# No weight remainders on GpSimd, ranks and weight addresses ahead of the row numbers, an own tile for the first two gathers

## The chip, the cores and the metric

The kernel runs on one core of one Trainium2 chip. The metric is device time in microseconds (us) of one execution. A profile gives the span of an execution too, which is a little shorter than its time. TensorE is called PE below, VectorE DVE, ScalarE ACT and GpSimd POOL, as in the profile; SP is the engine that issues most DMAs.

## The reference

Three stages follow each other: attention, a mixture of experts that sends every token to one expert, and a gated feed-forward block.

```python
# 1 attention: q, k, v are [2, 8, 576, 64]
scores = q @ k.T / 8
scores = where(scores >= max(scores) - tau, scores, -1e9)
x = (softmax(scores) @ v)              # heads joined: 1152 tokens x 512

# 2 mixture of experts: 8 experts, w1 [8, 512, 1024], w2 [8, 1024, 512]
logits = x @ w_gate                    # 1152 x 8
e = argmax(logits); gate = softmax(logits)[e]
# each expert takes its tokens in order, up to `capacity` (288)
y = relu(x_e @ w1[e]) @ w2[e]
x = gate * y[back at the token's place]     # dropped tokens are 0

# 3 feed-forward
out = (silu(x @ w_gate2) * (x @ w_val)) @ w_out
```

## The kernel before

**Stages.** Attention ends near 165 us of the span, routing takes until about 175.8 us, the experts run until about 322 us and the feed-forward block takes the rest. Inside routing and the experts the order of instructions on PE, ACT, DVE and POOL is the order in which the code is written; only SP is left to a scheduler.

**Weights.** Every expert has four loads of 1 MB (`w1` group 0 and 1, `w2` group 0 and 1), issued by SP (`next_raw`) into a raw buffer. There are three buffers `raw` and, once the experts begin, two more `rawx`. Each load gives two pieces. `next_piece` takes a piece from the raw buffer into one of six slots `ring`, as two float32r halves: the high part is a rounded copy (`split_hi`, line 220 on ACT or 218 on POOL), the low part is what the rounding left (`finish`, line 312, source minus high part, on DVE or POOL). A low part on DVE is put off until the next call; after the second piece of a load its buffer is free and SP may fill it again. The table `POOLED` names pieces whose two halves POOL makes: `w2` pieces 1 and 3 of experts 1 and 2, four pieces.

**Experts 0, 1 and 2.** Experts are taken in order of their token counts, the smallest first: expert 0 with 64 rows, 1 and 2 with 128, the others with more. For 1 and 2 (`expert_rows`, line 1443) PE does eight products of six matmuls of 512 columns each, one per piece: four with `w1`, then four with `w2`. Between them it turns the hidden rows (`turn`: ACT copies `hb` out of PSUM, PE transposes, ACT and DVE write the two parts of `ht`), turns the result of the expert before (`yb`, `yT`), and transposes one tile of gathered tokens at a time (`sort_tile`, line 1333, into `xsT`). After each product `next_piece` is called.

**Routing.** From the expert chosen for each of 1152 tokens (nine tiles of 128) the kernel needs four things.

- The place of each token in sorted order: `pos`, `dst`, `ndlo`, from prefix counts that PE adds up in `pt_`. The last matmul into `pt_` adds `gc`, the number of tokens of smaller experts.
- The tokens' row numbers `ids`: nine one-hot tables `olo` and nine matmuls into `ps_i`. Two gathers (indirect DMAs on POOL, line 1213) then fetch the first two tiles of sorted rows, into a raw buffer called `gbuf`, which goes back to the weights once both tiles are used; seven more gathers follow after the branch.
- Expert 0's 64 rows, without a gather: nine one-hot tables `hot` (lines 1159 to 1167, one on DVE, four on POOL, four on ACT) pick them by matmul into `ps_x0` (`pick_rows`, line 1178), eight matmuls in two groups per half of a tile.
- The rank of each expert (`rank`, `rm`, `vals`), which a matmul turns into `info`: which expert is the r-th and where its rows begin. SP reads `info` to address the weights of expert 1. From `info` also comes `slack`, on whose value all engines branch to one of several table widths (line 1773); and from `grhs` and a matmul into `ps_gt` comes `gat`, the gates in sorted order.

Of the kernel before, what the change touches and what calls it, by code (L numbers as in the profile page):

```python
# [10 lines left out]
F32 = mybir.dt.float32  # L11
# [12 lines left out]
def attention_moe_swiglu_kernel(  # L24
# [15 lines left out]
    nc = tc.nc  # L40
# [45 lines left out]
    XE = ()  # L86
    POOLED = tuple((e, "w2", g) for e in (1, 2) for g in (1, 3))
    MORE = ((1, 3), (2, 3))
# [22 lines left out]
    POLO = (8,)  # L111
    VH, PH, AH = (8,), (0,1,2,3), (4,5,6,7)
    SNAP = 1.5 * 2.0 ** 30
# [168 lines left out]

    slots, pooled = {}, set()

    def next_piece(lo_eng=None, hi_eng=None):
# [10 lines left out]
        if nm in ("w1", "w2"):  # L296
# [4 lines left out]
            if e in halves:  # L301
                src = t[:, (g % 2) * NPC:(g % 2 + 1) * NPC].rearrange("p (k f) -> p k f", k=kk)
            if (e, nm, g) in POOLED and pooled:
                lo_eng = hi_eng = nc.gpsimd
            lo_eng = lo_eng or nc.vector
# [831 lines left out]
    for a, (l, r_) in enumerate(rows_):  # L1137
# [5 lines left out]
                           op1=ALU.add)  # L1143
    V.scalar_tensor_tensor(out=gc, in0=krow, scalar=key[:, 0:1], in1=cntc.to_broadcast(T8),
                           op0=ALU.is_gt, op1=ALU.mult)
    pt_ = ps_r[:, 0:NTL * NE].rearrange("p (t e) -> p t e", t=NTL)
# [8 lines left out]
    mm(pt_[:, 0:M4], same, pre3, start=False, stop=False)  # L1155
    mm(pt_, onef, gc.unsqueeze(1).to_broadcast([NE, NTL, NE]), start=False, stop=True)
    V.tensor_scalar(out=npos, in0=p0_, scalar1=-1.0, scalar2=None, op0=ALU.mult)
    for t in VH:
        V.tensor_scalar(out=hot[:, t], in0=iot[:, 0:PK], scalar1=npos[:, t:t + 1],
                        scalar2=gm[:, t:t + 1], op0=ALU.is_equal, op1=ALU.mult)  # L1160
    for t in PH:
        nc.gpsimd.tensor_scalar(out=hot[:, t], in0=iot[:, 0:PK], scalar1=npos[:, t:t + 1],
                                scalar2=gm[:, t:t + 1], op0=ALU.is_equal, op1=ALU.mult)
    for i, t in enumerate(AH):
        nc.scalar.activation(out=sq[i], in_=iot[:, 0:PK], func=ACTF.Square, scale=-1.0,
                             bias=npos[:, t:t + 1])
        nc.scalar.activation(out=hot[:, t], in_=sq[i], func=ACTF.Relu, scale=ngm[:, t:t + 1],
                             bias=gm[:, t:t + 1])
    nc.scalar.activation(out=warm, in_=warm, func=ACTF.Silu)
    hord = list(VH) + [PH[0], AH[0], PH[1], AH[1], PH[2], PH[3], AH[2], AH[3]]  # L1170
    ps_x0 = sp.tile([128, 2, 512], F32, tag="s", name="ps_x0")
# [9 lines left out]

    pick_rows(hord[:RT1])
    V.tensor_tensor(out=pos, in0=pt_, in1=oh, op=ALU.mult)
# [15 lines left out]
    V.scalar_tensor_tensor(out=gt, in0=krow, scalar=key[:, 0:1], in1=onef[:, 0:NE], op0=ALU.is_lt,
                           op1=ALU.mult, accum_out=rank[:, 0:1])  # L1200
    V.scalar_tensor_tensor(out=gt, in0=krow, scalar=key[:, 0:1], in1=cntr, op0=ALU.is_lt,
                           op1=ALU.mult, accum_out=vals[:, 2:3])
    V.tensor_scalar(out=rm, in0=r8[0:NE], scalar1=rank[:, 0:1], scalar2=None, op0=ALU.is_equal)
    V.tensor_copy(out=vals[:, 0:1], in_=cntc)
    ps_i = mp.tile([128, 512], F32, tag="m", name="ps_i")
    ps_gt = mp.tile([128, 512], F32, tag="m", name="ps_gt")
    for x, t in enumerate(tord):
        mm(ps_i[:, 0:NTL], olo[t], rhs[:, t], start=x == 0, stop=x == NTL - 1)
    V.tensor_copy(out=ids, in_=ps_i[:, 0:NTL])
    gbuf = idle.popleft()  # L1210
    first = [gbuf[:, t * DM:(t + 1) * DM] for t in range(2)]
    for t in range(2):
        nc.gpsimd.indirect_dma_start(first[t], None, xd[:, :],
                                     bass.IndirectOffsetOnAxis(ap=ids[:, t:t + 1], axis=0))
    pick_rows(hord[RT1:RT1 + 1])
    mm(ps_c[0:3, 2 * NE:3 * NE], vals, rm)
    rr = ps_c[0:3, 2 * NE:3 * NE]
    V.tensor_copy(out=info[0:3], in_=rr)
    V.tensor_tensor(out=gp[:, :, 0], in0=gs, in1=gs, op=ALU.max)
    V.tensor_tensor(out=gm, in0=gs, in1=gp[:, :, 0], op=ALU.subtract)  # L1220
    V.tensor_tensor(out=gp[:, :, 1], in0=gm, in1=gm, op=ALU.max)
    V.tensor_tensor(out=gp[:, :, 2], in0=gm, in1=gp[:, :, 1], op=ALU.subtract)
    TG = [128, NTL, 3, NTL]
    V.tensor_tensor(out=grhs, in0=ohi.unsqueeze(2).to_broadcast(TG),
                    in1=gp.unsqueeze(3).to_broadcast(TG), op=ALU.mult)
    V.tensor_tensor(out=nd, in0=rr[0:1].unsqueeze(1).to_broadcast([1, 3, NE]), in1=wmax[0:1],
                    op=ALU.subtract)
    V.tensor_reduce(out=slack[0:1], in_=nd, axis=AX.X, op=ALU.max)
    pick_rows(hord[RT1 + 1:])
    for x, t in enumerate(tord):  # L1230
        mm(ps_gt[:, 0:3 * NTL], olo[t], grhs[:, t].rearrange("p v n -> p (v n)"), start=x == 0,
           stop=x == NTL - 1)
    expert_of(1)
    lim["raw"] += 1
    next_raw()
    for i in range(2):
# [22 lines left out]
    def rest(ctx, WS, drops):  # L1259
# [9 lines left out]
        slots.update(slots0)  # L1269
        pooled.clear()  # L1270
        halves.clear()
# [537 lines left out]
```

## Time and profile before

| what | value |
|---|---|
| median of 3 timed runs | 549.97 us (549.96 to 550.18) |
| the profiled execution | 549.28 us, span 547.2 us |
| TensorE busy | 527.9 us of the span (96%) |
| VectorE busy | 403.5 us (74%) |
| ScalarE busy | 297.5 us (54%) |
| GpSimd busy | 135.9 us (25%) |

The shares are means over stages. PE's few idle times are what can be won, so the rows to read are those of PE's waits, and from each wait the engine that released it. In a timeline row the numbers are the start, the duration and the operation, with the count where several are merged; a matmul's duration reaches past the start of the next one, since matmuls overlap. Where two instructions of one engine overlap in the records, the distance of their starts is what one costs.

### The profile page before, as it was taken

The numbers are of one execution on the slowest core, as the hardware profiler recorded it, in microseconds if no ns is written. First come the engines' busy times: TensorE is split into PE (matmuls) and PEld (weight loads), VectorE is DVE, ScalarE is ACT, GpSimd is POOL, SyncE is SP. The second block draws the span as 40 slices with busy tenths as digits, with TensorE's granted clock in tenths as the row PEclk, the third lists the DMA queues.
The fourth block names the chain that finished last, engine by engine and source line by source line (L and its number), as shares of the span: only waits on it lengthen the run. The fifth ranks groups of instructions, "written<-read, shape, count | busy, mean of one in ns | idle before, by whom it ended". The sixth has DMA issues, their size and how long they took to land. (4 is left out here: it accounts for less than half of the span.)

```text
span 547.2 us, 9914 instructions
## 1 busy us (share of the span) xinstructions
PE 527.9 (96%) x3654; PEld 476.5 (87%) x3655; DVE 403.5 (74%) x795; ACT 297.5 (54%) x575; POOL 135.9 (25%) x213
## 2 busy tenths in 40 slices
PE   7999999999998988999999999999999999999995
PEld 6877788787887766999999999999999999888884
DVE  5888989889976789888898968888885848622220
ACT  5886677767655777977787533243342224323221
POOL 6576193396555196100000000000000000011101
PEclk7899999999999999999999999999999999999998
DMA  6736345238203989976766152434421400001001
GB/s 187 226 70 133 83 116 127 77 80 248 98 17 96 388 327 330 300 236 227 237 219 216 44 203 78 153 90 143 153 82 73 156 2 0 1 38 40 28 30 44
DMA packets 61977, 73.82 MB, mean 135 GB/s; under 512 B 21216, under 2 KB 40288, under 8 KB 61920
## 3 DMA queue, kind: packets, MB, share of 16 engines
q1 hardware_dynamic: 60336, 68.38, 39.9%
q0 software_dynamic: 1440, 4.72, 2.3%
q8 instruction: 31, 0.51, 0.4%
q14 instruction: 26, 0.21, 0.1%
q10 hardware_dynamic: 144, 0.00, 0.0%
HBM read 63.06 MB, written 4.72 MB: 124 GB/s over the span
## 5 line engine op out<-in xcount | busy, mean ns | idle before, releaser
L1709 PE MATMUL pgv<-yT,ring 128*128 128x384 f32 x828 | 145.3, 337 | 0.0
L1709 PEld LDWEIGHTS pgv<-yT,ring 128*128 128x128 f32 x828 | 145.1, 188 | 0.0
L1762 POOL DMA_INDIRECT out_dram<-ob,ids x9 | 8.8, 975 | 313.4 <-ACT ob L1761 306.2
L220 ACT CAST ring<-raw 128x1024 fp32r<-128x1024 f32 x47 | 49.7, 1067 | 50.4 <-DVE raw L248 48.5
L713 ACT COPY pT<-ps_pt 128x512 f32<-128x512 f32 (+1 forms) x108 | 52.1, 485 | 39.3 <-PE ps_pt L709 39.3
L687 DVE SCALAR_TENSOR_TENSOR e<-s,th,e 128x576 f32<-128x576 f32 x72 | 58.7, 815 | 5.8 <-ACT e L676 3.9
L663 DVE TENSOR_REDUCE nm<-s 128x1 f32<-128x576 f32 x72 | 54.2, 753 | 9.3 <-PE s L653 9.0
L676 ACT ACTIVATE e<-s,nm 128x576 f32<-128x576 f32 x72 | 54.2, 753 | 3.3 <-DVE nm L663 3.1
L224 DVE TENSOR_TENSOR hs<-h,hs 128x768 fp32r<-128x768 f32 x18 | 17.2, 958 | 48.1 <-ACT hs L220 48.1
L312 DVE TENSOR_TENSOR ring<-raw,ring 128x1024 fp32r<-128x1024 f32 x33 | 47.0, 1441 | 4.7 <-PE ps_h L1519 2.4
L709 PE MATMUL ps_pt<-ident,e 128*128 128x128 f32 x324 | 48.0, 276 | 0.0
L1396 PE MATMUL ps_y<-h,ring 128*128 128x448 f32 (+3 forms) x144 | 41.7, 362 | 1.3 <-DVE h L1598 1.3
L1758 PE MATMUL po<-ring,hs 128*128 128x512 f32 x108 | 42.0, 389 | 0.0
L1757 PE MATMUL po<-ring,hs 128*128 128x512 f32 x108 | 42.0, 389 | 0.0
L1756 PE MATMUL po<-ring,hs 128*128 128x512 f32 x108 | 42.0, 389 | 0.0
L731 PE MATMUL ps_pv<-pT,v 128*64 128x256 f32 (+2 forms) x400 | 40.4, 328 | 0.0
L709 PEld LDWEIGHTS ps_pt<-ident,e 128*128 128x128 f32 x324 | 39.9, 143 | 0.2 <-issue 0.2
L220 ACT CAST ring<-rawx 128x1024 fp32r<-128x1024 f32 x25 | 26.4, 1055 | 22.4 <-DVE rawx L248 22.3
L1397 PE MATMUL ps_y<-h,ring 128*128 128x224 f32 (+3 forms) x144 | 35.8, 249 | 0.0
L1729 ACT ACTIVATE sg<-pgv 128x384 f32<-128x384 f32 x36 | 17.5, 485 | 29.7 <-PE pgv L1709 17.8
L1730 DVE TENSOR_TENSOR h<-sg,pgv 128x384 f32<-128x384 f32 x36 | 19.7, 549 | 17.9 <-PE pgv L1709 17.5
L1396 PE MATMUL ps_h<-xw,ring 128*128 128x448 f32 (+3 forms) x112 | 32.7, 362 | 0.0
(297 smaller groups left out, 1103.0 us busy)
## 6 DMA issues: line engine op xcount, KB each, us to landing
raw<-in_moe_w_dram SPq DMA_DIRECT2D x20, 1024.0 KB, 6.0
rawx<-in_moe_w_dram SPq DMA_DIRECT2D x12, 1024.0 KB, 5.5
raw<-in_moe_w_gate_dram SPq DMA_DIRECT2D x6, 1024.0 KB, 5.2
raw<-in_moe_w_out_dram SPq DMA_DIRECT2D x5, 1024.0 KB, 4.9
raw<-in_moe_w_val_dram SPq DMA_DIRECT2D x3, 1024.0 KB, 5.1
rawx<-in_moe_w_val_dram SPq DMA_DIRECT2D x3, 1024.0 KB, 5.1
k<-in_k_dram SPq DMA_DIRECT2D x8, 256.0 KB, 3.9
q<-in_q_dram SPq DMA_DIRECT2D x8, 256.0 KB, 4.1
```

The costliest lines, as they stand in the source:

```text
L220: nc.scalar.copy(dst, src)
L312: lo_eng.tensor_tensor(out=lo_, in0=src, in1=f32(hi_), op=ALU.subtract)
L663: nc.vector.tensor_reduce(out=nm_t[u][:, j:j + 1], in_=s_t[i][:, :, 0:SH], axis=AX.XY, op=ALU.max, negate=True)
L676: nc.scalar.activation(out=e_t[u][:, j].rearrange("p (a s) -> p a s", a=2), in_=s_t[i][:, :, 0:SH], func=ACTF.Exp, bias=nm_t[u][:, j:j + 1 ...
L687: nc.vector.scalar_tensor_tensor(out=ev, in0=s_t.pop(i)[:, :, 0:SH], scalar=th_t[u][:, j:j + 1], in1=ev, op0=ALU.is_ge, op1=ALU.mult, accu ...
L709: nc.tensor.transpose(ps[:, c * 128:(c + 1) * 128], ef[:, (c0 + c) * 128:(c0 + c + 1) * 128], ident)
L713: return lambda: nc.scalar.copy(pT[g][:, c0:c0 + m, o:o + 128], ps[:, 0:m * 128].rearrange("p (c t) -> p c t", c=m))
L1396: mm(ps[:, 0:2 * W], ws(wp, 0), x[:, 0:2 * W], start=first, stop=False)
L1709: mm(ps[:, 0:TH], (gw, vw)[w][:, i, kk, fl * 128:(fl + 1) * 128], yT[:, x, kk, th * TH:(th + 1) * TH], start=i + x + kk == 0, stop=i == 1 ...
L1756: mm(po, hs[:, 0, fl], ws[:, 0, sl], start=f == 0, stop=False)
L1757: mm(po, hs[:, 0, fl], ws[:, 1, sl], start=False, stop=False)
L1758: mm(po, hs[:, 1, fl], ws[:, 0, sl], start=False, stop=f == KF2 - 1)
```

## The change

Four edits.

- `POOLED` is gone: the four pieces of experts 1 and 2 are now made like all others, the high part on ACT and the low part on DVE.
- The ranks (`gt`, `rank`, `rm`) and the matmul that makes `info` stand ahead of `pos`; ACT copies `vals` and `info` out of PSUM. SP then loads two groups of expert 1's `w1` instead of one before the branch. `nd` and `slack` come ahead of the tables `olo`, and `grhs` ahead of the row numbers. The matmul that closes `pt_` stands behind the picks of three tiles.
- The first two gathers go into a tile of their own, `gfirst`, so no raw buffer is taken from the weights.
- Of the nine tables `hot` five are made on DVE (8, 3, 4, 5, 6), two on POOL (0, 1) and two on ACT (2, 7). The three parts `gp` of the gate move from DVE to POOL.

```diff
-    POOLED = tuple((e, "w2", g) for e in (1, 2) for g in (1, 3))
-    VH, PH, AH = (8,), (0,1,2,3), (4,5,6,7)
+    VH, PH, AH = (8, 3, 4, 5, 6), (0, 1), (2, 7)
+    gfirst = const.tile([128, 2, DM], F32, name="gfirst")
-            if (e, nm, g) in POOLED and pooled:
-                lo_eng = hi_eng = nc.gpsimd
...
-    V.scalar_tensor_tensor(out=gc, in0=krow, scalar=key[:, 0:1], in1=cntc.to_broadcast(T8),
-                           op0=ALU.is_gt, op1=ALU.mult)
+    nc.scalar.copy(vals[:, 0:1], cntc)
...
+    nc.gpsimd.tensor_scalar(out=gp[:, :, 0], in0=gs, scalar1=1.0, scalar2=1.0, op0=ALU.mult,
+                            op1=ALU.mult)
+    vhot(VH[0])
+    V.scalar_tensor_tensor(out=gt, in0=krow, scalar=key[:, 0:1], in1=onef[:, 0:NE], op0=ALU.is_lt,
+                           op1=ALU.mult, accum_out=rank[:, 0:1])
+    V.scalar_tensor_tensor(out=gt, in0=krow, scalar=key[:, 0:1], in1=cntr, op0=ALU.is_lt,
+                           op1=ALU.mult, accum_out=vals[:, 2:3])
+    V.tensor_scalar(out=rm, in0=r8[0:NE], scalar1=rank[:, 0:1], scalar2=None, op0=ALU.is_equal)
+    vhot(VH[1])
+    V.scalar_tensor_tensor(out=gc, ...)
+    for t in VH[2:]:
+        vhot(t)
...
-    hord = list(VH) + [PH[0], AH[0], PH[1], AH[1], PH[2], PH[3], AH[2], AH[3]]
+    hord = [VH[0], PH[0], AH[0], VH[1], VH[2], VH[3], PH[1], VH[4], AH[1]]
...
+    ahot(0)
+    pick_rows(hord[:1])
+    mm(rr, vals, rm)
+    nc.scalar.copy(info[0:3], rr)
+    expert_of(1)
+    lim["raw"] += 2
+    next_raw()
+    next_raw()
+    for i in range(1, len(AH)):
+        ahot(i)
+    nc.scalar.activation(out=warm, in_=warm, func=ACTF.Silu)
+    pick_rows(hord[1:3])
+    mm(pt_, onef, gc.unsqueeze(1).to_broadcast([NE, NTL, NE]), start=False, stop=True)
+    pick_rows(hord[3:])
     V.tensor_tensor(out=pos, in0=pt_, in1=oh, op=ALU.mult)
...
-    gbuf = idle.popleft()
-    first = [gbuf[:, t * DM:(t + 1) * DM] for t in range(2)]
+    first = [gfirst[:, t] for t in range(2)]
...
-            if t == NG0 - 1:
-                idle.append(gbuf)
-                next_raw()
```

How the instructions stand on the engines, at three places. `spare` is the memory that holds the small tables of routing (`hot`, `olo`, `npos`, `pos`, `ndlo` and others).

DVE in routing before, from `gc` to the tables `olo`: L1157 is `npos`, L1159 the one table `hot`, L1183 `pos`, L1197 `olo`.

```order
L1144 SCALAR_TENSOR_TENSOR gc<-krow,key,ps_c 8x8
L1157 TENSOR_SCALAR spare_2453<-ps_p 128x9
L1159 TENSOR_SCALAR spare_2452<-iot,spare_2453 128x64
L1183 TENSOR_TENSOR spare_2453<-ps_r,spare_2453 128x72
L1184 TENSOR_REDUCE spare_2453<-spare_2453 128x9
L1185 TENSOR_SCALAR spare_2453<-spare_2453 128x9
L1186 SCALAR_TENSOR_TENSOR spare_2453<-spare_2453 128x9
L1188 TENSOR_TENSOR spare_2453<-spare_2453,ioh 128x81
L1193 TENSOR_TENSOR rhs<-spare_2453,tokf 128x81
L1197 TENSOR_SCALAR spare_2452<-iot,spare_2453 128x128 x8
```

The same place now; L1216 is `pos`, L1159 the five tables `hot`.

```order
L1154 TENSOR_SCALAR spare_2454<-ps_p 128x9
L1159 TENSOR_SCALAR spare_2453<-iot,spare_2454 128x64
L1163 SCALAR_TENSOR_TENSOR gt,rank<-krow,key,onef 8x8
L1165 SCALAR_TENSOR_TENSOR gt,vals<-krow,key,ps_c 8x8
L1167 TENSOR_SCALAR rm<-r_78,rank 8x8
L1159 TENSOR_SCALAR spare_2453<-iot,spare_2454 128x64
L1169 SCALAR_TENSOR_TENSOR gc<-krow,key,ps_c 8x8
L1159 TENSOR_SCALAR spare_2453<-iot,spare_2454 128x64 x3
L1216 TENSOR_TENSOR spare_2454<-ps_r,spare_2454 128x72
L1217 TENSOR_REDUCE spare_2454<-spare_2454 128x9
L1218 TENSOR_SCALAR spare_2454<-spare_2454 128x9
```

Four more tables, the three rank instructions and `gc` now stand between `npos` and `pos`, where one table stood.

ACT in expert 1 before, from the scaling of a gathered tile to the copy of the second `ht`.

```order
L1322 ACTIVATE g<-g,gat 128x512
L1456 CAST ht<-ps_ht 128x512
L220 CAST ring_102<-raw_103 128x1024
L1462 ACTIVATE hb<-ps_h 128x512
L1456 CAST ht<-ps_ht 128x512
```

The same place now.

```order
L1332 ACTIVATE g<-g,gat 128x512
L220 CAST ring_102<-rawx_2718 128x1024
L1463 CAST ht<-ps_ht 128x512
L220 CAST ring_103<-rawx_2717 128x1024
L1469 ACTIVATE hb<-ps_h 128x512
L220 CAST ring_98<-rawx_2717 128x1024
L1463 CAST ht<-ps_ht 128x512
```

A cast of a piece stands ahead of each `ht` copy now; in expert 2 likewise one stands ahead of the first `hb`, one ahead of the second. DVE has four low parts more at the matching places.

POOL in the experts before, from the memset of `xsT` on.

```order
L1377 MEMSET xsT 128x4x80
L1312 DMA g<-xd,ids 128x512 x4
L218 TENSOR_SCALAR ring_101<-rawx_2719 128x1024
L312 TENSOR_TENSOR ring_101<-rawx_2719,ring_101 128x1024
L218 TENSOR_SCALAR ring_97<-raw_103 128x1024
L312 TENSOR_TENSOR ring_97<-raw_103,ring_97 128x1024
L1312 DMA g<-xd,ids 128x512
```

POOL now, from the last part of `gp` to the gathers of the experts.

```order
L1179 TENSOR_TENSOR gp<-spare_2454,gp 128x9
L1224 TENSOR_SCALAR spare_2453<-iot,spare_2454 128x128
L1244 DMA gfirst<-xd,ids 128x512 x2
L1258 TENSOR_LOAD slack
L1780 COMPARE_AND_BRANCH
L1387 MEMSET xsT 128x4x80
L1322 DMA g<-xd,ids 128x512 x7
```

POOL has nothing but the gathers left in the experts.

## Rows read from the trace of the kernel before

**Rows 1.** view by stretches: busy us (count) per engine, granted clock, DMA share, GB/s
```profile
270.00:330.00 60.00, 60.00 (x412) 58.55 (x411) 49.91 (x91) 34.75 (x72) 0.00 (x0) 1.00 0.50 167
```

**Rows 2.** PE's waits, 195 to 222 us: us in total, times, longest us
```profile
PE ps_y L1443 <- POOL ring L312: 1.6, 2, 1.3
PE ps_y L1443 <- DVE ring L312: 1.5, 1, 1.5
PE ps_h L1443 <- DVE ring L312: 0.4, 1, 0.4
```

**Rows 3.** timeline of PE in experts 1 and 2: start us, us, operation, [idle before <-releaser]
```profile
186.85 1.57 PE L1443 MATMUL ps_h<-ring,xw 128*128 128x512 f32 x6
199.71 0.71 PE L1443 MATMUL ps_y<-ring,ht 128*128 128x512 f32 x2
201.72 1.19 PE L1443 MATMUL ps_y<-ring,ht 128*128 128x512 f32 x4 [1.30 <-POOL ring L312]
```

**Rows 4.** timeline of DVE from expert 0 to expert 2
```profile
183.61 0.48 DVE L1325 TENSOR_SCALAR raw<-raw,gat 128x512 f32<-128x512 f32 x1
185.13 1.23 DVE L312 TENSOR_TENSOR ring<-raw,ring 128x1024 fp32r<-128x1024 f32 x1 [0.51 <-ACT ring L220]
194.58 3.39 DVE L312 TENSOR_TENSOR ring<-raw,ring 128x1024 fp32r<-128x1024 f32 x1 [0.26 <-ACT ring L220]
199.36 9.84 DVE L312 TENSOR_TENSOR ring<-raw,ring 128x1024 fp32r<-128x1024 f32 x4
209.72 2.64 DVE L312 TENSOR_TENSOR ring<-rawx,ring 128x1024 fp32r<-128x1024 f32 x1
212.88 2.81 DVE L312 TENSOR_TENSOR ring<-rawx,ring 128x1024 fp32r<-128x1024 f32 x1
```

**Rows 5.** timeline of GpSimd in the same stretch
```profile
194.50 2.39 POOL L312 TENSOR_TENSOR ring<-rawx,ring 128x1024 fp32r<-128x1024 f32 x1
211.36 3.24 POOL L312 TENSOR_TENSOR ring<-rawx,ring 128x1024 fp32r<-128x1024 f32 x1
```

**Rows 6.** timeline of ScalarE in expert 1
```profile
193.01 0.59 ACT L1456 CAST ht<-ps_ht 128x512 fp32r<-128x512 f32 x1 [0.19 <-PE ps_ht L1452]
193.49 1.05 ACT L220 CAST ring<-raw 128x1024 fp32r<-128x1024 f32 x1
194.46 0.60 ACT L1462 ACTIVATE hb<-ps_h 128x512 f32<-128x512 f32 x1
```

**Rows 7.** timeline of all engines through routing
```profile
168.66 0.31 DVE L1159 TENSOR_SCALAR spare<-iot,spare 128x64 f32<-128x64 bf16 x1
168.67 2.48 POOL L1162 TENSOR_SCALAR spare<-iot,spare 128x64 f32<-128x64 bf16 x4 [0.67 <-DVE spare L1157]
169.01 0.23 DVE L1183 TENSOR_TENSOR spare<-ps_r,spare 128x72 f32<-128x72 f32 x1
169.55 0.40 PE L1178 MATMUL ps_x<-spare,xk 128*64 128x64 f32 x8
169.78 0.40 PE L1178 MATMUL ps_x<-spare,xr 128*64 128x64 f32 x8
170.29 1.42 DVE L1197 TENSOR_SCALAR spare<-iot,spare 128x128 f16<-128x128 bf16 x8
172.88 1.21 POOL L1213 DMA_INDIRECT raw<-xd,ids  x1 [0.97 <-DVE ids L1209]
174.15 0.41 DVE L1224 TENSOR_TENSOR grhs<-spare,gp 128x243 bf16<-128x243 f32 x1
175.84 3.00 PE L1519 MATMUL ps_h<-ring,x 128*128 128x512 f32 x12 [0.83 <-DVE gat L1243]
```

**Rows 8.** gathers of tiles 2 to 8, last line of the view of their tile
```profile
DMA to landing us min/median/max: 5.8/6.5/6.6
```

**Rows 9.** weight loads of line 192, last line of the view of that line
```profile
DMA to landing us min/median/max: 6.2/8.3/11.9
```

**Rows 10.** PE's waits, 222 to 262 us: us in total, times, longest us
```profile
PE ps_y L1396 <- DVE h L1598: 1.3, 2, 0.8
```

More of the change, by code (lines that the diff above doesn't have):

```diff
@@ L281, in finish_piece @@
             late.pop()()
-    slots, pooled = {}, set()
+    slots = {}
     def next_piece(lo_eng=None, hi_eng=None):
@@ L1088, in attention_moe_swiglu_kernel @@
     npos, gm, ngm, gs = [rt_(n, [128, NTL]) for n in ("npos", "gm", "ngm", "gs")]
+    gr = rt_("gr", [128, NTL])
     gp = rt_("gp", [128, NTL, 3], BF16)
@@ L1155, in attention_moe_swiglu_kernel, with vhot @@
     mm(pt_[:, 0:M4], same, pre3, start=False, stop=False)
-    mm(pt_, onef, gc.unsqueeze(1).to_broadcast([NE, NTL, NE]), start=False, stop=True)
     V.tensor_scalar(out=npos, in0=p0_, scalar1=-1.0, scalar2=None, op0=ALU.mult)
-    for t in VH:
+    nc.gpsimd.tensor_scalar(out=gp[:, :, 0], in0=gs, scalar1=1.0, scalar2=1.0, op0=ALU.mult,
+                            op1=ALU.mult)
+    def vhot(t):
         V.tensor_scalar(out=hot[:, t], in0=iot[:, 0:PK], scalar1=npos[:, t:t + 1],
                         scalar2=gm[:, t:t + 1], op0=ALU.is_equal, op1=ALU.mult)
+    vhot(VH[0])
[5 more added lines that the diff above has]
+    vhot(VH[1])
+    V.scalar_tensor_tensor(out=gc, in0=krow, scalar=key[:, 0:1], in1=cntc.to_broadcast(T8),
+                           op0=ALU.is_gt, op1=ALU.mult)
+    for t in VH[2:]:
+        vhot(t)
     for t in PH:
@@ L1163, in attention_moe_swiglu_kernel, with ahot @@
                                 scalar2=gm[:, t:t + 1], op0=ALU.is_equal, op1=ALU.mult)
-    for i, t in enumerate(AH):
+    nc.gpsimd.tensor_tensor(out=gr, in0=gs, in1=gp[:, :, 0], op=ALU.subtract)
+    nc.gpsimd.tensor_scalar(out=gp[:, :, 1], in0=gr, scalar1=1.0, scalar2=1.0, op0=ALU.mult,
+                            op1=ALU.mult)
+    nc.gpsimd.tensor_tensor(out=gp[:, :, 2], in0=gr, in1=gp[:, :, 1], op=ALU.subtract)
+    ps_i = mp.tile([128, 512], F32, tag="m", name="ps_i")
+    rr = ps_i[0:3, 64:64 + NE]
+    def ahot(i):
+        t = AH[i]
         nc.scalar.activation(out=sq[i], in_=iot[:, 0:PK], func=ACTF.Square, scale=-1.0,
@@ L1168, in attention_moe_swiglu_kernel @@
                              bias=gm[:, t:t + 1])
-    nc.scalar.activation(out=warm, in_=warm, func=ACTF.Silu)
-    hord = list(VH) + [PH[0], AH[0], PH[1], AH[1], PH[2], PH[3], AH[2], AH[3]]
+    hord = [VH[0], PH[0], AH[0], VH[1], VH[2], VH[3], PH[1], VH[4], AH[1]]
     ps_x0 = sp.tile([128, 2, 512], F32, tag="s", name="ps_x0")
@@ L1180, in pick_rows @@
                        stop=t == hord[-1] and kk % 2 == 1)
-    pick_rows(hord[:RT1])
+    ahot(0)
[12 more added lines that the diff above has]
+    pick_rows(hord[3:])
     V.tensor_tensor(out=pos, in0=pt_, in1=oh, op=ALU.mult)
@@ L1193, in attention_moe_swiglu_kernel @@
     V.tensor_tensor(out=rhs, in0=ohi, in1=tokf.unsqueeze(2).to_broadcast(T9), op=ALU.mult)
+    V.tensor_tensor(out=nd, in0=rr[0:1].unsqueeze(1).to_broadcast([1, 3, NE]), in1=wmax[0:1],
+                    op=ALU.subtract)
+    V.tensor_reduce(out=slack[0:1], in_=nd, axis=AX.X, op=ALU.max)
     tord = [t for t in range(NTL) if t not in POLO] + list(POLO)
@@ L1198, in attention_moe_swiglu_kernel @@
                             op0=ALU.is_equal)
[L1199 to L1205, printed above, removed]
+    TG = [128, NTL, 3, NTL]
+    V.tensor_tensor(out=grhs, in0=ohi.unsqueeze(2).to_broadcast(TG),
+                    in1=gp.unsqueeze(3).to_broadcast(TG), op=ALU.mult)
     ps_gt = mp.tile([128, 512], F32, tag="m", name="ps_gt")
@@ L1214, in attention_moe_swiglu_kernel @@
                                      bass.IndirectOffsetOnAxis(ap=ids[:, t:t + 1], axis=0))
[L1215 to L1229, printed above, removed]
     for x, t in enumerate(tord):
@@ L1232, in attention_moe_swiglu_kernel @@
            stop=x == NTL - 1)
-    expert_of(1)
-    lim["raw"] += 1
-    next_raw()
     for i in range(2):
@@ L1269, in rest @@
         slots.update(slots0)
-        pooled.clear()
         halves.clear()
@@ L1285, in rest @@
         packed = WS[0] == PK
-        if packed:
-            pooled.add(1)
         if WS in (FAST, PACK):
@@ L1418, in sort_now @@
                 sort_scale(t + 1)
-            if t == NG0 - 1:
-                idle.append(gbuf)
-                next_raw()
             if t == 0 and packed:
```

## The prediction

> **What bounds the kernel now.** I read the busy shares first: PE works nearly all of the span, so time is won only where PE stands still. The stretches show where: from 270 to 330 us PE is busy for 60.00 of 60 us [rows 1], so work behind the first experts moves as a whole when its start moves. The list of PE's waits by stretch then names the idle time in experts 1 and 2: 1.6 us on low parts of pieces made by POOL, 1.5 and 0.4 us on low parts made by DVE, 3.5 us in all [rows 2]. No other stretch of the experts has as much; experts 3 and 4 have 1.3 us together [rows 10].
>
> The timeline of PE says how much a wait costs. Six matmuls of a product take 1.57 us with the tail of the last and two of them 0.71 [rows 3], so four more cost 0.86, and one, with the gap between groups, about 0.24 us. The two at 199.71 should have been followed at 200.19; the next started at 201.72, so 1.53 us were lost where 1.30 are shown as idle [rows 3], the difference being the tail. There are four such breaks. Idle time plus four tails of 0.2 gives 4.3 us, and that is the prize in this stretch.
>
> Why are the parts late? On DVE a low part takes 1.23 us at 185.13, but 3.39 at 194.58, 9.84 for four from 199.36, 2.64 and 2.81 later [rows 4]. The stretched parts lie beside POOL's own low parts, which take 2.39 to 3.24 us [rows 5]. Against 1.23 each the seven stretched parts cost 2.2 + 4.9 + 1.4 + 1.6 = 10.1 us. So the four pieces given to POOL save DVE four low parts (4.9 us) and cost it 10.1.
>
> The Trainium skill (SBUF — State Buffer, Who interferes with whom) says that a DVE instruction with two SBUF inputs contends with a GpSimd instruction that reads SBUF, and that the loser stands still for the whole instruction. The row at 194.58 agrees, since it ends about one low part after POOL's at 194.50 does. The same section speaks against another part of this change, taken up below.
>
> **The change part by part.**
>
> *No pieces on POOL.* DVE is rid of 10.1 us of slowing and gets 4.9 us of low parts, so in experts 1 and 2 it has 5.2 us less to do. ACT gains four casts; a cast costs 0.97 us, a copy in front of it 0.48, by the distance of their starts [rows 6], so 3.9 us more. Per expert ACT then has eight casts (7.8 us), about eight half-microsecond copies (3.8), and by my estimate 1.5 us of scaling and `xw`, two or three operations somewhat longer than a copy: 13.1 us. PE needs per expert 48 matmuls at 0.24 and some 2.3 us of transposes (five groups of four, at the same pace per column and with gaps, an estimate): 13.8 us. ACT is under PE, but close, and in order: a cast in front of a copy that PE waits for delays it by up to 0.97. I went through expert 1 and 2 in the new order with these costs, starting from the rows at 193 us. In expert 1 the first `ht` copy comes 0.6 us later than in the row at 193.01, which PE's third and fourth products cover; the second has slack. In expert 2 the two `hb` copies come behind a cast that was not there, and PE, ready to transpose, waits 0.5 and 0.3 us. So of 4.3 us lost 0.8 stay: **-3.5 us**. Bounds: 0 stays (-4.3), or all four casts fall on PE (3.9 stay, -0.4). I take the value of the walk, since until 195 us PE had no wait though ACT made nearly every cast.
>
> *Ranks, tables and addresses.* PE starts expert 0 at 175.84, 1.28 us after the end of `grhs` at 174.56 [rows 7]; the copies into `x0` and the branch lie in this. So what counts is when `grhs` ends. `pos` started at 169.01. It now waits for the matmul that closes `pt_`, behind the picks of tiles 8, 0 and 2 and the rank matmul. A tile is two groups 0.23 us apart [rows 7]; from 169.0 three tiles make 1.4, the small matmuls some 0.5, so `pos` starts at 170.9 to 171.0, 2.0 us later. DVE's own queue is no later: four more tables at 0.24 (between the 0.18 of an `olo`, 1.42 for eight, and the 0.31 shown for a `hot` [rows 7]), the ranks and `gc` make about 1.8, so the tables hide there. From `pos` to the first `olo` are 1.28 us as before, plus 0.35 for `nd` and `slack` (one small operation is 0.23 or less [rows 7]); eight `olo` 1.42; `grhs` 0.41 follows at once instead of behind five small copies. That ends at 171.0 + 1.28 + 0.35 + 1.42 + 0.41 = 174.46: **-0.1 us**. Bounds: if `pos` follows DVE's queue alone -0.6; if each of the inserted operations costs its full 0.31 and none hides, +1.0.
>
> *Later gathers.* The row numbers come behind `grhs`, at 174.4 instead of 172.4, so the first gather starts near 174.9 instead of 172.88 [rows 7], the second near 176.4. Gathers under full weight traffic land 5.8 to 6.6 us after issue [rows 8], so the second tile is there by 183.0. DVE scales it at 183.61 [rows 4]. Cost 0, with 0.6 us of cover; the first is due at 181.1 and may hold DVE for some tenths, before an idle of DVE. Bounds 0 and +1.
>
> *Earlier weights and `gfirst`.* SP issues 2 MB near 171 us instead of 1 MB at 174.4, and no buffer waits for the gathered tiles. Among the waits of ACT and DVE from 175 to 235 us none is on a load, so this gives 0. It lengthens the lead of the loads, which covers the faster pace.
>
> *Behind.* Expert 3 begins with DVE less behind, by 0.3 us in the walk; of the 1.3 us [rows 10] I take 0.2 back: **-0.2 us** (-0.8 to +0.5, the latter if ACT's lag is carried over).
>
> Sum: -3.5 - 0.1 - 0.2 = -3.8 us. The profiled execution took 549.28 us (span 547.2), so 545.5; the median of the runs shown is 549.97, 0.7 above it. With the same distance the median of the changed kernel is **546.2 us**.
>
> **The rivals.**
>
> *ACT becomes the bound.* ACT has 13.1 us of work per expert against PE's 13.8, and copies for PE stand behind casts. Halfway between the 0.8 of the walk and the 3.9 of the bound, 2.3 us stay: -2.0 - 0.1 - 0.2 = -2.3, so 547.7, from 547 to 549.3. For it: ACT's low margin. Against: ring slots are four pieces ahead of PE.
>
> *DVE's tables wait for POOL's.* If DVE's `hot` tables had to take turns with POOL's two, DVE would stand still twice for 0.62 us (2.48 for four [rows 7]), 1.2 us, of which the 0.2 hide by which `pos` waits for PE anyway: +1.0, so 547.2. Against: eight `olo` ran on DVE at 0.18 each from 170.29 while POOL's four `hot` lasted from 168.67 to 171.15 [rows 7]. The skill's section named above gives this outcome, since it lets `tensor_scalar` into the contending modes; the row of `olo` disagrees with it.
>
> *The rows of the second tile land late: slower.* Up to 4 MB of weights are now issued ahead of the gathers. Expert 1 cannot start before the second tile is scaled, transposed and copied, which took from 183.61 [rows 4] to 186.85 [rows 3]. If that gather takes 12 us, as the slowest weight load of this stretch did (11.9 [rows 9]), it lands at 188.4, expert 1 starts 4.9 us late, and with -3.8 the time is 551.1. It decides from a landing 11 us after issue on. Against: no gather took more than 6.6 [rows 8].
>
> *It does not do what it says.* If the stretched low parts came from the weight traffic and not from POOL, the 4.3 us would stay and only -0.1 and -0.2 be left: 549.7. Against: 1.23 at 185.13, in the midst of the loads too [rows 4].
>
> *More than forecast.* No stall stays, routing gains 0.6 and expert 3 0.8: -5.7, 544.3.
>
> **How the numbers follow.** Forecast 0.56, its own range 545.2 to 547.2; ACT 0.19, a quarter of it above 548.9; DVE and POOL in turns 0.07; late gather 0.08; no effect 0.05; more than forecast 0.05. About 0.2% (1.1 us) is what a measurement of this kernel tells from no change. Faster: 0.56 + 0.14 + 0.07 + 0.05 = 0.82; within: 0.05 + 0.05 = 0.10; slower 0.08. The range from 544.6 to 549.1 leaves out the late gather, the case without effect and the ends of two others.
>
> **What would show it.** Right: every low part on DVE near 1.2 us between 190 and 222 us; no PE wait on `ring`; short PE waits on `hb` or `ht` copies of ACT in expert 2; expert 0 starting within 0.6 us of 175.8; expert 3 starting 3.6 us earlier. Wrong: waits of PE or DVE on a gathered tile, waits of ACT on a weight load, `pos` far behind 171 us, or PE waits in expert 3 grown by more than the gain.

## The result and the profile after

The changed kernel takes 545.24 us (median of four runs, 545.22 to 545.51) where the kernel before takes 549.97 on the same chip: a ratio of 0.9916, 95% interval 0.9899 to 0.9933. Forecast were 546.2 us. The profiled executions differ by 4.06 us (549.28 and 545.22), their spans by 3.9 (547.2 and 543.3).

The timeline of TensorE, cut at four marks, says where. The marks are the first matmul of the prefix sums (the routing begins), the first of expert 0, the first of expert 1 and the first matmul of 144 columns in expert 3. In the rows the columns are start, duration, engine, line, operation, tiles, shape, count and the idle time in front. The marks after:

```profile
168.14 0.29 PE L1152 MATMUL ps_r<-osb,masks 128*128 128x32 bf16 x6
175.97 2.98 PE L1526 MATMUL ps_h<-ring,x 128*128 128x512 f32 x12 [0.70 <-DVE gat L1256]
186.96 1.55 PE L1450 MATMUL ps_h<-ring,xw 128*128 128x512 f32 x6
215.39 0.23 PE L1407 MATMUL ps_h<-xw,ring 128*128 128x144 f32 x1
```

Of before, the two marks that the rows ahead of the prediction don't have (the others are 175.84 [rows 7] and 186.85 [rows 3]):

```profile
168.13 0.29 PE L1154 MATMUL ps_r<-osb,masks 128*128 128x32 bf16 x6
218.87 0.23 PE L1397 MATMUL ps_h<-xw,ring 128*128 128x144 f32 x1
```

The differences of neighbouring marks, in us, and of the same marks in the profile of every experiment told below:

| kernel | ratio | routing | expert 0 | experts 1 and 2 | from expert 3 to the end |
|---|---|---|---|---|---|
| before | 1 | 7.71 | 11.01 | 32.02 | 328.3 |
| after | 0.9916 | 7.83 | 10.99 | 28.43 | 327.9 |
| after, repeated | 0.9909 | 7.83 | 12.68 | 28.44 | 327.9 |
| only the remainders off GpSimd | 0.993 | 7.71 | 11.01 | 28.40 | 327.9 |
| all but that | 1.003 | 7.74 | 12.49 | 32.00 | 328.0 |
| own tile, remainders off GpSimd | 0.9922 | 9.02 | 12.10 | 28.41 | 327.9 |
| GpSimd reads beside | 1.0089 | 8.35 | 12.29 | 36.64 | 328.1 |
| GpSimd writes beside | 0.9961 | 8.23 | 12.07 | 28.44 | 328.2 |
| high parts on GpSimd | 0.9923 | 7.83 | 10.99 | 28.74 | 328.2 |
| two casts on VectorE | 0.9881 | 7.78 | 11.53 | 28.26 | 328.1 |
| the same, sum of ranks early | 0.9882 | 7.12 | 12.03 | 28.31 | 328.0 |
| the same, addresses late | 0.9898 | 7.13 | 11.60 | 29.57 | 328.2 |
| after, addresses late | 0.9917 | 7.77 | 11.95 | 28.87 | 328.2 |

So of the 3.9 us of span 3.59 come from experts 1 and 2, and the routing gives 0.1 away. The 0.4 of the last column is hardly work saved: from the fourth mark to TensorE's last matmul (at 541.17 before, at 537.63 after) it is 322.30 us before and 322.24 after, and the rest passes between the last matmul and the end of the span, 6.0 us before and 5.7 after. In all profiles of this table this tail lies between 5.6 and 6.0 us.

The list of TensorE's waits from 172 to 232 us after (engine, what it waited for and who releases it: us in total, times, longest):

```profile
PE ps_y L1406 <- DVE h L1605: 0.8, 1, 0.8
PE ps_h L1526 <- DVE gat L1256: 0.7, 1, 0.7
PE ps_y L1526 <- DVE ht L1549: 0.5, 1, 0.5
PE ps_ht L1459 <- ACT hb L1469: 0.4, 1, 0.4
```

The waits for `ring` [rows 2] are gone; in experts 1 and 2 the list has one wait of 0.4 us for ScalarE's copy `hb` left. VectorE's low parts after:

```profile
194.97 2.35 DVE L310 TENSOR_TENSOR ring<-rawx,ring 128x1024 fp32r<-128x1024 f32 x2
199.81 4.75 DVE L310 TENSOR_TENSOR ring<-raw,ring 128x1024 fp32r<-128x1024 f32 x4
209.68 1.22 DVE L310 TENSOR_TENSOR ring<-rawx,ring 128x1024 fp32r<-128x1024 f32 x1 [0.21 <-ACT ring L220]
```

Four in a row take 4.75 us where four took 9.84 [rows 4]: 1.2 each, the duration of one with GpSimd idle.

The routing after, VectorE's tables `hot` and `pos`, GpSimd's tables beside them, the matmul that closes the sum of ranks, and the first gather:

```profile
169.90 0.74 DVE L1159 TENSOR_SCALAR spare<-iot,spare 128x64 f32<-128x64 bf16 x3
168.61 1.18 POOL L1174 TENSOR_SCALAR spare<-iot,spare 128x64 f32<-128x64 bf16 x2 [0.41 <-DVE spare L1154]
170.97 0.44 PE L1214 MATMUL ps_r<-gc,onef 8*128 8x72 f32 x2
171.45 0.23 DVE L1216 TENSOR_TENSOR spare<-ps_r,spare 128x72 f32<-128x72 f32 x1 [0.81 <-PE ps_r L1214]
174.43 0.40 DVE L1236 TENSOR_TENSOR grhs<-spare,gp 128x243 bf16<-128x243 f32 x1
175.27 1.21 POOL L1244 DMA_INDIRECT gfirst<-xd,ids  x1 [2.20 <-DVE ids L1241]
```

VectorE stands still for 0.81 us ahead of `pos`, which starts 2.44 us later than the 169.01 of before [rows 7]; `grhs` ends at 174.83 instead of 174.56.

### The profile page after: what moved, and what is told of

Same layout as the page of the kernel before. It is cut to its first block, busy times and chain, and to the rows that moved or that the text cites. A ratio compares the mean times of both kernels' runs of the same rounds, so it can differ in the third digit from the quotient of the medians.

```text
span 543.3 us, 9910 instructions
## 1 busy us (share of the span) xinstructions
PE 527.9 (97%) x3655; PEld 477.0 (88%) x3655; DVE 398.2 (73%) x797; ACT 299.4 (55%) x577; POOL 118.7 (22%) x207
## 5 line engine op out<-in xcount | busy, mean ns | idle before, releaser
L220 ACT CAST ring<-raw 128x1024 fp32r<-128x1024 f32 x49 | 51.8, 1065 | 62.1 <-DVE raw L248 60.1
L310 DVE TENSOR_TENSOR ring<-raw,ring 128x1024 fp32r<-128x1024 f32 x36 | 43.6, 1220 | 4.1 <-PE ps_h L1526 2.4
L220 ACT CAST ring<-rawx 128x1024 fp32r<-128x1024 f32 x27 | 28.7, 1063 | 10.7 <-DVE rawx L248 10.7
```

The lines of the kernel that those rows point to most:

```text
L220: nc.scalar.copy(dst, src)
L310: lo_eng.tensor_tensor(out=lo_, in0=src, in1=f32(hi_), op=ALU.subtract)
```

## The experiments

Three theories stood against each other for the 3.6 us. The theory of reads: GpSimd's reads of SBUF stretched VectorE's low parts, and TensorE waited for these and for GpSimd's own. The theory of loads: weight traffic stretched them, and the earlier loads and the own tile cured it. The theory of lateness: GpSimd's own pieces came late, and its work beside VectorE did no harm. The letters in the expectations are those of each experiment by itself.

One part of the time differs between executions whatever the edit. From 13 to 18 us, long before the change, four matmuls of `s` take either 1.30 or 0.76 us; of before, and of the first experiment:

```profile
13.33 1.30 PE L653 MATMUL s<-kp,ring 128*128 128x288 f32 x4 [0.70 <-DVE th L671]
```

```profile
13.02 0.76 PE L653 MATMUL s<-kp,ring 128*128 128x288 f32 x4 [0.82 <-DVE th L671]
```

The routing then begins at 168.0 to 168.3 us, or at 166.2 to 166.6. Of 22 runs of the kernel before on the first experiments' chip, ten took 547.15 to 547.46 us and twelve 548.64 to 549.59, the same distance apart. That the two are one thing is likely, not shown. Ratios of the experiments that lie within 0.3% of each other are therefore not ranked here; the stages in the table are.

Expert 0 differs by a second thing, TensorE's clock. In three of the profiles (own tile, GpSimd reads, GpSimd writes) the granted clock fell to 0.50, the lower of its two levels (1.2 GHz), within the first twelve matmuls of expert 0. TensorE had stood before it for 2.14 us in the first, for 0.80 and 0.63 us in the second, for 0.66 and 0.60 us in the third. The twelve matmuls then took 4.28, 4.58 and 4.57 us, where they take 3.00 before [rows 7] and 2.98 after. Of the own tile, the matmuls and the view by stretches (columns as in [rows 1]: the clock is the third number from the end):

```profile
175.59 4.28 PE L1516 MATMUL ps_h<-ring,x 128*128 128x512 f32 x12 [2.14 <-DVE gat L1243]
178.00:180.00 2.00, 2.00 (x8) 1.62 (x6) 0.85 (x2) 1.53 (x2) 1.55 (x1) 0.50 1.05 391
```

In none of the three does TensorE wait for a gathered tile; the wait of 0.5 us for `ht` that after has in expert 0 is 0.3 us or gone. So what their expert 0 (12.07 to 12.29 us) lasts longer is the clock's, and no row shows a cost of the edit in it.

**Only the remainders off GpSimd.** The kernel before with one line changed:

```diff
-    POOLED = tuple((e, "w2", g) for e in (1, 2) for g in (1, 3))
+    POOLED = ()
```

> The kernel before with an empty table of POOL's pieces, and nothing else of the change. Theory (the gain is the end of POOL's four pieces): 545.3 to 546.3 us, DVE low parts of 1.23 us throughout experts 1 and 2, no PE wait on a piece, one PE wait of about 0.4 us on ScalarE's hb in expert 2. Rival (the gain comes from the earlier weights, the free raw buffer or the new routing): 549 us or more.

Measured: ratio 0.993 (0.9911 to 0.9949). Low parts at 1.2 us, no wait for `ring`, and experts 1 and 2 in 28.40 us. This one line has the whole gain of that stretch, with the old routing and the old loads. The theory of loads falls.

**All the rest of the change.** The changed kernel with the four pieces back on GpSimd:

```diff
-    POOLED = ()
+    POOLED = tuple((e, "w2", g) for e in (1, 2) for g in (1, 3))
```

> The changed kernel with the four pieces given back to POOL; routing, addresses, gfirst and tables as changed. Theory: within 0.5 us of the kernel before (549.5 to 550.5), with the 3.5 us of PE idle on low parts back. Rival: 546 to 547, the stalls not coming back since the weights are earlier.

Measured: ratio 1.003 (1.0009 to 1.0051). The waits for pieces are back as they were [rows 2], and a new one stands in expert 0; TensorE's waits:

```profile
PE ps_y L1456 <- POOL ring L313: 1.6, 2, 1.3
PE ps_y L1456 <- DVE ring L313: 1.5, 1, 1.5
PE ps_g L1349 <- DVE gfirst L1341: 1.3, 1, 1.3
```

So the rest of the change gives nothing by itself and can cost: TensorE waited 1.3 us for the first gathered tile, and expert 0 lasted 12.49 instead of 11.01 us.

**GpSimd reads beside.** The changed kernel; where GpSimd used to convert a piece, it now works on a scratch tile that nobody needs (set once ahead of the branch):

```diff
+            if (e, nm, g) in POOLED and pooled:
+                w = wts[0]
+                nc.gpsimd.tensor_scalar(out=w, in0=w, scalar1=1.0, scalar2=1.0, op0=mult, op1=mult)
+                nc.gpsimd.tensor_tensor(out=w, in0=w, in1=w, op=subtract)
```

> The changed kernel, and at the four places where POOL made a piece before, POOL copies and subtracts a 128x1024 scratch tile in place (reading and writing SBUF); nobody waits for it. Theory (DVE low parts are stretched by POOL instructions that read SBUF): low parts beside them take 2.4 to 3.4 us again, and 1 to 3 us of PE waits on low parts made by DVE come back: 546 to 548. Rival (PE lost its time because POOL itself was late with its pieces): low parts stay at 1.23 and the time at 545.2.

Measured: ratio 1.0089 (1.006 to 1.0118). VectorE's low parts and GpSimd's work beside them:

```profile
195.07 4.59 DVE L316 TENSOR_TENSOR ring<-rawx,ring 128x1024 fp32r<-128x1024 f32 x2
203.02 7.16 DVE L316 TENSOR_TENSOR ring<-raw,ring 128x1024 fp32r<-128x1024 f32 x4
```

```profile
194.69 1.90 POOL L308 TENSOR_TENSOR wt<-wt 128x1024 f32<-128x1024 f32 x1
205.23 2.74 POOL L308 TENSOR_TENSOR wt<-wt 128x1024 f32<-128x1024 f32 x1
```

Two low parts take 4.59 us where two took 2.35, four 7.16 where four took 4.75. Nothing waits for GpSimd's result here, so the theory of lateness falls: VectorE is stretched by what GpSimd does beside it. (That GpSimd's own pieces came late as well is in [rows 2], 1.6 us.) Experts 1 and 2 last 36.64 us, 8.2 more than after and 4.6 more than before: VectorE now has the stretching and all the low parts. The mechanism was expected, its size not, because a late VectorE then holds `ht` back too, and because the granted clock fell to 0.50 again (from 221 to 223 us) when TensorE had stood for 2.46 us. Eight matmuls took 3.64 us there, eight others 2.09 at 205.91, so some 1.5 of the 8.2 us are the clock's:

```profile
219.63 3.64 PE L1460 MATMUL ps_y<-ring,ht 128*128 128x512 f32 x8 [2.46 <-DVE ht L1474]
```

TensorE's waits:

```profile
PE ps_y L1460 <- DVE ht L1474: 2.7, 2, 2.5
PE ps_y L1460 <- DVE ring L316: 2.2, 3, 1.2
PE ps_h L1460 <- DVE ring L316: 1.1, 1, 1.1
```

**GpSimd writes beside.** As the last, with memsets of the scratch tile only:

```diff
+                for _ in range(4):
+                    nc.gpsimd.memset(wts[0], 0.0)
```

> As the run with POOL's scratch copies, but with four memsets of the same tile per place, which write SBUF and read none of it. Theory (only POOL instructions that read stretch a DVE instruction with two SBUF inputs): low parts stay near 1.23 us, 545.2 to 545.7. Rival (any POOL work beside stretches them): 2.4 to 3.4 us again and the time as in the run with the copies.

Measured: ratio 0.9961 (0.9944 to 0.9977). GpSimd is busy at the same four places, and VectorE's low parts do not notice:

```profile
194.74 8.08 POOL L306 MEMSET wt<- 128x1024 f32 x8
204.34 4.01 POOL L306 MEMSET wt<- 128x1024 f32 x4
```

```profile
196.32 2.35 DVE L314 TENSOR_TENSOR ring<-rawx,ring 128x1024 fp32r<-128x1024 f32 x2
201.17 4.75 DVE L314 TENSOR_TENSOR ring<-raw,ring 128x1024 fp32r<-128x1024 f32 x4
```

Experts 1 and 2 last 28.44 us, as after. So it is GpSimd's reading that stretches VectorE's low parts, not its being busy. What the kernel loses against after lies ahead. In expert 0 (12.07 us) it is the clock, as told above. In the routing (8.23 us for 7.83) it is the memset that sets the scratch tile, in front of the gathers and beside the last of VectorE's tables `olo`:

```profile
173.02 2.11 DVE L1237 TENSOR_SCALAR spare<-iot,spare 128x128 f16<-128x128 bf16 x8
174.09 0.96 POOL L1271 MEMSET wt<- 128x1024 f32 x1 [1.13 <-PE ps_x L1202]
```

After has these eight in 1.37 us (at 173.13). Here they end at 175.13, with the memset, which ends at 175.05; the longest took 1.10 us where the median is 0.24. The kernel with reads, which sets its tile in the same way, has the same delay in its routing (8.35). So for these tables, with one tensor input, a write of GpSimd was enough.

**High parts on GpSimd.** The changed kernel, the four high parts cast by GpSimd (`hi_eng = nc.gpsimd`), the low parts by VectorE.

> The changed kernel, but of the four w2 pieces of experts 1 and 2 that GpSimd used to convert, it again writes the high part (a cast, one SBUF input), and VectorE the low part. Theory A (what cost the time was VectorE's low parts beside GpSimd's two-input subtraction and the waits for GpSimd's own low parts; the high part on ScalarE cost next to nothing): ScalarE's hb wait of 0.4 us goes, but GpSimd's cast takes about 2 us against ScalarE's 1.05, so that low parts of VectorE come later; the time stays within 1 us of the changed kernel. Rival B (any GpSimd read of SBUF holds VectorE's two-input subtractions up by what it lasts): VectorE's low parts beside the casts go from 1.23 to 2 us and more, PE waits 1 to 2 us in experts 1 and 2, and the time is 1 to 3 us over the changed kernel's. Rival C (ScalarE was what remained): 0.4 us faster.

Measured: ratio 0.9923 (0.9891 to 0.9954), experts 1 and 2 in 28.74 us, 0.3 more than after. GpSimd's cast has one SBUF input, and still:

```profile
194.47 3.20 DVE L313 TENSOR_TENSOR ring<-rawx,ring 128x1024 fp32r<-128x1024 f32 x2
199.93 5.46 DVE L313 TENSOR_TENSOR ring<-raw,ring 128x1024 fp32r<-128x1024 f32 x4
208.79 3.68 DVE L313 TENSOR_TENSOR ring<-rawx,ring 128x1024 fp32r<-128x1024 f32 x2
```

against 2.35, 4.75 and 2.35 for as many alone: 0.7 to 1.3 us per cast of 1.05 us. The wait for ScalarE's `hb` goes, one of 0.7 us for VectorE's `ht` takes its place. The time is as theory A has it, within 1 us of after; the mechanism of rival B is there all the same, at a smaller price. Rival C is out.

**Two casts on VectorE.** The changed kernel, the high parts of expert 2's two pieces cast by VectorE.

> The changed kernel, but the high parts of two of the four pieces, those of expert 2, are cast by VectorE and not by ScalarE. Theory A (after the change ScalarE is late by 0.4 us once, in expert 2, and VectorE has room there): the wait of TensorE for hb goes, VectorE's two casts of some 0.7 to 1.2 us fit, the time falls by 0.4 us. Rival B (VectorE has no room between its low parts): the wait for hb is replaced by one for ring of 0.5 to 1 us, the time rises by as much.

Measured: ratio 0.9881 (0.9858 to 0.9905), experts 1 and 2 in 28.26 us, and the list has no wait of TensorE from 182 to 222 us. The sign is theory A's, with 0.17 us instead of 0.4. The waits for `hb` go, but in expert 2 six matmuls take 1.93 us where after has 1.52, and eighteen 4.78 where after has 4.37:

```profile
206.74 1.93 PE L1456 MATMUL ps_y<-ring,ht 128*128 128x512 f32 x6
207.20 0.68 DVE L1470 TENSOR_TENSOR ht<-ps_ht,ht 128x512 fp32r<-128x512 f32 x1
```

In each a pause of about 0.4 us ends 0.06 us behind VectorE's second part of `ht` (at 207.94, and again at 211.54). So VectorE had room for a part only: rival B's mechanism with another tile than it named, at less than the gain.

**The sum of ranks early as well.** `gc` right behind the first table, and the closing matmul right behind the first pick:

```diff
     vhot(VH[0])
+    V.scalar_tensor_tensor(out=gc, in0=krow, scalar=key[:, 0:1], ...)
...
     pick_rows(hord[:1])
+    mm(pt_, onef, gc.unsqueeze(1).to_broadcast([NE, NTL, NE]), start=False, stop=True)
```

> As the run before, and in the routing the set gc is built right behind the first hot table and the matmul that closes the sum of ranks stands right behind the first pick, ahead of the second, so that pos can start 0.4 to 0.8 us sooner than at 171.45. Theory A (pos waits for the closing matmul, which waits for gc and stands behind other matmuls): gathers start 0.4 us sooner; expert 0 starts 0.3 to 0.5 us sooner than in the changed kernel; together 0.7 us below it. Rival B (the olo comparisons and grhs that follow pos wait for the one-hot sets of GpSimd anyway): expert 0 starts when it did, and the time is that of the run before.

Measured: ratio 0.9882 (0.9854 to 0.991). The routing lasts 7.12 us instead of 7.78, so `pos` did wait for the closing matmul for nothing. But TensorE then waits 0.8 us for `gfirst`, and of the 0.66 us that the routing won 0.50 are lost in expert 0: the bound had moved to the landing of the first gather, which neither theory had named.

**Addresses late.** Two kernels, the changed one and the last one, with the weight addresses taken behind the row numbers:

```diff
-    nc.scalar.copy(info[0:3], rr)      # ahead of the picks
...
     V.tensor_copy(out=ids, in_=ps_i[:, 0:NTL])
+    V.tensor_copy(out=info[0:3], in_=rr)
```

> The changed kernel, but the weight addresses are copied by VectorE behind the row numbers, as before, so that the two weight loads are issued behind the two gathers. In the repeat of the changed kernel two loads of 1 MB were issued at 171.31, the gathers at 175.35 and 176.86, the first of them landed 8.2 us later and TensorE waited 1.4 us for it. Theory A (the early loads fill the DMA engines when the gathers come): the gathers land in 5 to 6 us as before, no wait for gfirst, and the time is 0 to 1.4 us below the changed kernel's, 0.7 in the mean. Rival B (the early loads feed a ring that would otherwise be late): a wait for raw or ring of 0.5 us or more appears in expert 0 or 1 and the time rises by it. Rival C (the landing varies by itself): gathers land 6 to 8 us as in the changed kernel, no difference.

> The version with two casts on VectorE and the early closing matmul (expert 0 0.7 us sooner, of which a wait of 0.8 us for the first gather took the whole back), now with the weight addresses behind the row numbers. Theory A: the wait of 0.8 us for gfirst goes and the 0.7 us are kept: ratio 0.986 to 0.987 to the kernel before, the best so far. Rival B: the weight loads, later by 3 us, make ring late: ratio 0.988 or more.

Measured: 0.9917 (0.9895 to 0.9938) and 0.9898 (0.9879 to 0.9917). The wait moves from the first gathered tile to the second and stays (0.7 and 0.4 us). In both kernels ScalarE now waits for weight loads (2.4 and 2.9 us from 175 to 200), and in the second TensorE waits 1.0 us for ScalarE:

```profile
PE ps_yt L1540 <- ACT hb L1545: 1.0, 1, 1.0
PE ps_g L1349 <- DVE gfirst L1341: 0.4, 1, 0.4
```

So putting the loads behind the gathers does not pay. For the second kernel rival B holds; in the first its mechanism is there, at 0.2 us of TensorE. That the early loads alone make the gathers late is not shown.

**The own tile without the new routing.** The kernel before without remainders on GpSimd, with `gfirst`.

> The kernel before, without remainders on GpSimd and with the own tile for the first two gathers, with the old order of the routing. It differs from the first experiment (0.993) by the own tile alone. Theory A (the own tile frees a weight buffer that the kernel did not wait for): ratio 0.993, no difference. Rival B (a weight load more in flight beside the gathers holds them up): the gathers land later by 1 us or more, TensorE waits for them, and the ratio is 0.994 to 0.996. Rival C (a load sooner helps): 0.991.

Measured: ratio 0.9922 (0.9904 to 0.9939), not to be told from the 0.993 without the tile. Its gathers landed 3.7 us after issue and nobody waited for them: rival B is out, and nothing speaks for rival C. Its profile has a pause of 2.1 us ahead of expert 0 in which TensorE stood (the copies of ScalarE into `x0` started at 174.40, though the picks had ended at 172.6); no row names a cause, and it stays open. Behind it the clock fell, as told above.

**After, repeated.** The changed kernel beside three of these (high parts on GpSimd, two casts on VectorE, the sum of ranks early).

> The changed kernel once more, as the yardstick for the three beside it. Every theory: ratio 0.9916 to the kernel before, experts 1 and 2 in 28.2 us without a wait for a piece, one wait of TensorE for ScalarE's hb of 0.4 us.

Measured: ratio 0.9909 (0.9879 to 0.9939), six runs from 543.99 to 548.64 us. Experts 1 and 2 as before, but in the profiled execution the first gather landed late. Of after, and of the repeat, the line of the DMA issues (count, median us from issue to landing):

```profile
gfirst<-xd,ids POOLq DMA_INDIRECT x2, 6.3
```

```profile
gfirst<-xd,ids POOLq DMA_INDIRECT x2, 8.2
```

and TensorE's wait in the repeat:

```profile
PE ps_g L1343 <- DVE gfirst L1335: 1.4, 1, 1.4
```

SP had issued two loads of 1 MB at 171.31, ahead of the gathers at 175.35 and 176.86; so it had in the execution without the wait:

```profile
171.24 1.09 SPq L187 DMA_DIRECT2D raw<-in_moe_w_dram  x2
```

## Why the prediction was right, point by point

- **No pieces on POOL, -3.5: right.** Experts 1 and 2 are 3.59 us shorter, and 3.6 in each of the pairs that differ by the pieces alone (32.02 and 28.40 with the old routing, 32.00 and 28.43 with the new). The cause that the prediction named is shown by the two experiments with GpSimd reading and writing beside. Of the stalls 0.8 us stay, as the walk left them, if they are counted as the prediction counts, by the distance of starts. The first `hb` wait of expert 2 cost 0.55 us for 0.5: twelve matmuls and the transposes behind them start 3.41 us apart (202.83 and 206.24), where it was 2.86 before. The second, which the list of waits does not show, cost 0.27 for 0.3: six matmuls and the transposes start 1.64 us apart (208.56 and 210.20), where it was 1.37 before (194.20 and 195.57):

```profile
206.24 0.66 PE L1459 MATMUL ps_ht<-ident,hb 128*128 128x128 f32 x4 [0.42 <-ACT hb L1469]
208.56 1.52 PE L1450 MATMUL ps_y<-ring,ht 128*128 128x512 f32 x6
210.20 0.66 PE L1459 MATMUL ps_ht<-ident,hb 128*128 128x128 f32 x4
```

- **The Trainium skill** (SBUF — State Buffer, Who interferes with whom) has it that a two-input VectorE instruction contends with GpSimd where that reads SBUF and not where it only writes. Both halves agree with the rows: 2.35 for two became 4.59 beside reads and stayed 2.35 beside memsets.
- **Routing, -0.1: the sign failed, by 0.2 us.** It lost 0.12. The step that failed is the start of `pos`: 171.45 and not 170.9 to 171.0, since the closing matmul came at 170.97 and `pos` half a microsecond behind it. The prediction let TensorE run through the picks and small matmuls; but the matmul of the ranks needs `rm` from VectorE, which ended at 169.62, and it began at 169.77, 0.28 us later than the picks in front of it allow. The loss stayed small because expert 0 now begins 1.14 us after `grhs`, not 1.28.
- **Later gathers, 0: right in the profiled execution, wrong as a rule.** VectorE waited 0.3 us for the first tile, TensorE none. But the prediction gave the cover of the second tile (0.6 us) and let the first one off with "some tenths", on landings of 5.8 to 6.6 us from one execution [rows 8]. The landings of the first two gathers run from 3.6 to 8.2 us over the experiments, and 8.2 cost 1.7 us (expert 0 in 12.68 instead of 10.99): more than the bound of +1. The tile that decides is the first: at 175.27 + 6.3 its rows come at 181.6, they are scaled in 0.49 us, and TensorE takes them at 182.4, so there were 0.3 us to spare. The price begins near a landing of 6.6 us and not at 11, as the rival had it; with two casts on VectorE a landing of 7.0 us left TensorE idle for 0.3, and expert 0 lasted 0.54 longer than after.
- **Earlier weights and `gfirst`, 0: right for the own tile**, whose two kernels can't be told apart by their ratios. For the addresses it is open: they gain nothing, and with them late the gathers still hold TensorE up for 0.7 us.
- **Expert 3, -0.2: did not come.** The two waits, 1.3 us together [rows 10], are there unchanged. They wait for `h`, and what VectorE had less behind it did not shorten them:

```profile
PE ps_y L1406 <- DVE h L1605: 1.3, 2, 0.8
```

- **The sum.** On its own execution -3.8 was forecast and -4.06 came, but not all of it by the change. Up to TensorE's last matmul 3.54 us were won: expert 3 and the routing took 0.4 back, and experts 1 and 2 gave 0.1 more than forecast. The other half microsecond passed between the last matmul and the end of the execution, where no edit stands. That the two sums lie so close is in this part luck.
- **To the median, +0.7: the mis-sized term.** The profiled execution of before lay 0.69 below its median, that of after 0.02. Carrying this distance over made 0.7 of the 1.0 us by which the forecast missed; the rest is the 0.26 of the sum.
- **The rivals.** ScalarE as the bound: 0.8 us stayed, not 2.3; taking two casts off it won 0.17, since VectorE was late in its place. VectorE's tables in turns with GpSimd's: VectorE's took 0.25 each (0.74 for three), GpSimd's 0.59 each (1.18 for two), against 0.62 before, so they ran side by side, and the reading of that section of the Trainium skill by which `tensor_scalar` takes turns does not hold for these tables. It was a memset that held tables up, in the two kernels with a scratch tile. No effect: out with the first experiment. Late gather: it exists, at a third of its price.

The best versions run are those with two casts on VectorE, 0.9881 and 0.9882. In the same comparison the changed kernel has 0.9909 with an overlapping interval, so they beat the kernel before for certain and the changed one only by their stages: 0.17 us in experts 1 and 2, and 0.7 in the routing as long as the first gather does not take it back.

## What to carry to other kernels

Before giving a second elementwise engine a share of the work, compare the duration of the first engine's instruction beside it and alone: here the helper took over 4.9 us of work and cost 10.1. When a change makes one step ready sooner, look at what the next step waits for in that moment, and at the transfer with the least cover, not the last one. A cover of half a microsecond on a transfer seen once is a chance, not a zero. And before a longer stage is put down to an edit, compare the time of the same matmuls and the granted clock in it: here three stages were a microsecond longer by the clock alone.

## What the runs showed of the hardware

- GpSimd's own duration varies in the same neighbourhood: a subtraction of 128x1024 took it 1.90 to 2.75 us in the experiment with reads, and 2.39 to 3.24 in the kernel before [rows 5]. How long one takes with VectorE idle was not run.
- A GpSimd memset of 128x1024 (0.96 us) left VectorE's two-input subtractions at 1.2 us each, but held up its tables of 128x128 (bf16 to f16, one tensor input): eight took 2.11 us instead of 1.37. Beside GpSimd's own tables eight had taken 1.42 [rows 7].
- A GpSimd cast with a single SBUF input also stretches VectorE's two-input subtraction, by 0.7 to 1.3 us for a cast of 1.05.
- The granted clock fell to 0.50 behind stops of TensorE in the four places told above (2.14 us; 0.80 and 0.63; 0.66 and 0.60; 2.46), and at the last of them eight matmuls took 3.64 us instead of 2.09. In the kernel before TensorE stood for 0.43 and 0.83 us ahead of expert 0, and the clock stayed at 1.00.
- A gather of 128 rows under the same weight loads landed after 6.3 us in one execution of a kernel and after 8.2 in another.
- In the stretch from 13 to 18 us the granted clock was 0.51 in the profile of before and 1.00 in that of after, while four matmuls of `s` took 1.30 us in both, and 0.76 in other executions at 1.00. There the clock that is recorded does not say how fast the matmuls ran. Of before and of after, the view by stretches:

```profile
13.00:18.00 5.00, 4.67 (x24) 4.67 (x24) 3.63 (x11) 3.17 (x7) 4.66 (x15) 0.51 0.59 132
```

```profile
13.00:18.00 5.00, 4.62 (x25) 4.62 (x25) 3.63 (x11) 3.17 (x7) 4.66 (x14) 1.00 0.53 119
```
